# Filter rows for the upper partitions: four loads replaced by two engine copies in a kernel's prologue, and the weights' load issued earlier

## The chip, the cores and the metric

The kernel runs on one core of one Trainium2 chip. The metric is the device time in microseconds; lower is better. A run's time is some 1.8 us longer than the span of its profile (783.67 against 781.9 us in the profile). Times before come from runs of 782.77 to 784.03 us.

## The reference

```python
def _attn_ref(x, filt_r, filt_i):          # x: 8 x 3008 x 256
    X = np.fft.rfft(x, axis=1)
    Y = X * (filt_r + 1j * filt_i)[None]
    return np.fft.irfft(Y, n=x.shape[1], axis=1).astype(np.float32)

def _moe_ref(x, w_in, w_out):              # 24064 x 256, 256 x 2048, 2048 x 256
    h = x @ w_in
    return (np.maximum(0.01 * h, h) @ w_out).astype(np.float32)

# reference: _moe_ref(_attn_ref(x, ...).reshape(24064, 256), ...)
```

A filter along the sequence by Fourier transform, then two dense layers with a leaky ReLU between.

## The kernel before

The transforms are matmuls with small constant matrices in several stages: first stage, a transpose on the vector engine (STREAM_TRANSPOSE in the profiles, single ones of 128x1024 took 1.22 and 1.25 us), second stage, product with the filter, third stage, a second transpose, fourth stage. The dense layers follow. The batches 1 to 7 are transformed while the dense layers of an earlier batch run. Only batch 0 stands alone: it is the **prologue**, some 42 us in which TensorE has nothing else to do. Batch 0 is worked in two halves of 128 columns (`hf`).

The filter lies in `fa_sb` (real part) and `fb_sb` (imaginary part). Both halves of the partitions need the same rows, so rows 0 to 63 ("lower") are repeated in 64 to 127 ("upper"). For half 0 two engine copies do that (`upper(0)`); for half 1 the kernel before loads the rows from DRAM a second time. In code and profiles, PE is TensorE, DVE or `dve` the vector engine, ACT or `act` the scalar engine, Pool the GpSimd engine and SP SyncE, which here only issues DMAs. A load "lands" when its data has arrived.

```python
    def filt_load(dst, src, d0, dn, up=0):
        for q, first, sgn in ((0, 0, 1), (Q, N1, -1)):
            nc.gpsimd.dma_start(dst[up + q : up + q + Q, :, ds(d0, dn)], ...)
    ...
    for hf in range(2):
        filt_load(fa_sb, filt_r, hf * DH, DH)
        filt_load(fb_sb, filt_i, hf * DH, DH)
    filt_load(fa_sb, filt_r, DH, DH, 64)         # upper rows of half 1
    filt_load(fb_sb, filt_i, DH, DH, 64)
    ...
    def first_s2(hf, c, n, kind, on_pool=False): # second stage and products, n columns of rows
        ps = bank(kind, n, DH)
        ...                                      # matmuls into ps
        if on_pool:
            ...                                  # ACT copies ps to SBUF, Pool multiplies
        else:
            for i in range(2):                   # by fa, then by fb
                nc.vector.tensor_tensor(y[i], ps, fs[i], AL.mult)

    def first_sa(hf, c, n=4):                    # third stage, evacuated by ACT
        ...
    def upper(hf):
        for t, cp in ((fa_sb, act), (fb_sb, dve)):
            cp(t[64:P, :, ts(hf, DH)], t[0:64, :, ts(hf, DH)])
    ...
    t1_part(0, 0, True)(), t1_part(0, 1, True)() # first transposes
    nc.vector.memset(i1_sb[:, 0, 0:2], 0.0)
    nc.sync.dma_start(i1_sb[:], i1_d.ap())       # inverse constants, 752 KB
    upper(0)
    first_s2(0, 8, 8, "ph", True)
    nc.gpsimd.dma_start(w_in_sb[:], ...)         # first-layer weights
    t1_part(0, 2, True)()
    first_s2(0, 0, 8, "ph")
    for n0 in (0, N2 // 2):
        x_load(1, n0, N2 // 2)
    t1_part(0, 3, True)()
    first_s2(0, 16, 4, "pf"), first_s2(0, 20, 4, "pf")
    keep_warm(4)                                 # idle matmuls
    first_s2(1, 0, 8, "ph")
    first_sa(0, 0, 8)
    first_s2(1, 8, 8, "ph", True)
    nc.gpsimd.dma_start(w_out_sb[:], ...)
    first_sa(0, 16), first_sa(0, 20), first_sa(0, 8, 8)
    first_s2(1, 16, 4, "pf"), first_s2(1, 20, 4, "ph")
    first_sa(1, 0, 8)
    ...                                          # rest of third stage, transposes, fourth stage
```

## Time and profile before

| | kernel before |
|---|---|
| median of 3 runs | 782.98 us (782.77 to 784.03) |
| span of the profile | 781.9 us |
| TensorE busy | 770.7 us, 99% |
| first vector transpose starts | 17.48 us |
| first dense-layer matmul starts | 42.40 us |
| from there to the end | 739.5 us |

Two marks of this table serve throughout. The first transpose of the vector engine starts when the input of batch 0 has come in and gone through the first stage, and that moment moves by itself. I call the time from the first transpose to the first dense-layer matmul the **lead-in**: 42.40 - 17.48 = 24.92 us here.

### The profile page before, as it was taken

How to read it: one execution, taken by the hardware profiler on the slowest of the kernel's cores; microseconds unless marked ns; L12 is line 12 of the kernel's file. 1: busy time of each engine (PE TensorE's matmuls, PEld its weight loads, DVE VectorE, ACT ScalarE, POOL GpSimd, SP SyncE). 2: the span in 40 equal slices, each digit the busy share in tenths (PEclk: the TensorE clock that was granted, in tenths of full speed). 3: DMA queues.
4: the chain of work that ended last, by engine and by line, in shares of the span. 5: the costliest groups of instructions: out<-in, count | busy, mean ns of one | idle time of the engine just before them, and what ended most of it. 6: DMA issues, size and time to landing. Idle time of an engine off the chain costs nothing.

```text
span 781.9 us, 13405 instructions
## 1 busy us (share of the span) xinstructions
PE 770.7 (99%) x5710; PEld 523.5 (67%) x5710; DVE 368.6 (47%) x467; ACT 550.7 (70%) x783; POOL 150.2 (19%) x124
## 2 busy tenths in 40 slices
PE   8799999999999999999999999999999999999998
PEld 4366677666776667666777667766677666766666
DVE  4879751865237641577307754087432765200000
ACT  4586769676787767777587775967668776666664
POOL 5963300340004300042001410025000340000000
PEclk9999999999999999999999999999999999999999
DMA  9973102301041101510105010140101001110111
GB/s 182 220 112 75 38 28 57 93 28 41 29 106 42 42 28 42 108 41 29 41 28 122 28 39 31 41 107 28 42 28 42 28 28 41 41 37 32 41 41 55
DMA packets 39500, 44.16 MB, mean 56 GB/s; under 512 B 11282, under 2 KB 37522, under 8 KB 38674
## 3 DMA queue, kind: packets, MB, share of 16 engines
q0 software_dynamic: 13104, 17.01, 13.2%
q1 hardware_dynamic: 26336, 26.30, 9.6%
q8 instruction: 44, 0.72, 0.4%
q14 instruction: 16, 0.13, 0.1%
HBM read 35.67 MB, written 24.64 MB: 77 GB/s over the span
## 4 chain that ended last, share of the span: by engine, by line
PE 94%; DMA 3%; ACT 1%; DVE 1%; POOL 1%; issue 0%; DVEq 0%; POOLq 0%
PE ph L377 41%; PE po_ps L391 41%; DMA fb_sb<-in_filt_i_dram 3%; PE pf L174 3%; PE pf L241 2%; PE pf L229 2%; PE pf L214 2%; PE pf L391 1%; ACT big L185 0%; DVE prod L281 0%; DVE big L296 0%; POOL x_sb L132 0%; ACT yt L308 0%; PE ph L305 0%; ACT gt_c L382 0%
## 5 line engine op out<-in xcount | busy, mean ns | idle before, releaser
L382 ACT ACTIVATE gt_c<-ph 128x1024 f16<-128x1024 f32 x376 | 385.3, 1025 | 195.3 <-PE ph L377 194.0
L377 PE MATMUL ph<-yt,w_in_sb 128*128 128x512 f16 (+3 forms) x1600 | 386.4, 366 | 0.3
L391 PE MATMUL po_ps<-w_out_sb,gt_c 128*128 128x256 f16 x2944 | 381.5, 272 | 0.5 <-ACT ost_c_t L398 0.5
L391 PEld LDWEIGHTS <-gt_c 128*128 128x128 f16 x3008 | 290.8, 98 | 89.2 <-issue 1.9
L377 PEld LDWEIGHTS <-w_in_sb 128*128 128x128 f16 x1600 | 154.5, 98 | 95.7 <-issue 0.4
L222 POOL TENSOR_TENSOR y_b_g<-p_b_g,p_b_g 128x512 f16<-128x512 f32 x84 | 106.9, 1273 | 225.0 <-DVE p_b_g L220 225.0
L197 DVE STREAM_TRANSPOSE big<-big 128x1024 f32<-128x1024 f32 x32 | 55.9, 1850 | 126.1 <-ACT big L185 126.1
L185 ACT CAST big<-pf 128x512 f16<-128x512 f32 x186 | 106.4, 603 | 1.8 <-PE pf L254 1.8
L244 DVE CAST yt<-pf 128x376 f16<-128x376 f32 x112 | 56.3, 544 | 86.1 <-PE pf L241 86.1
L218 DVE TENSOR_TENSOR p_b_g<-pf,fa_sb 128x512 f32<-128x512 f32 x84 | 58.1, 692 | 37.7 <-PE pf L214 34.9
L398 ACT COPY ost_c_t<-po_ps 128x256 f32<-128x256 f32 x184 | 69.3, 377 | 6.5 <-PE po_ps L391 5.3
L205 DVE STREAM_TRANSPOSE big<-big 128x1024 f32<-128x1024 f32 x28 | 51.0, 1934 | 34.4 <-ACT big L185 34.4
L219 DVE TENSOR_TENSOR p_b_g<-pf,fb_sb 64x512 f32<-64x512 f32 x84 | 58.2, 692 | 1.1
L220 DVE TENSOR_TENSOR p_b_g<-pf,fb_sb 64x512 f32<-64x512 f32 x84 | 57.4, 683 | 1.1
L132 POOL DMA_DIRECT2D x_sb<-in_x_dram x13 | 7.1, 546 | 254.9 <-PE pf L174 254.1
L241 PEld LDWEIGHTS <-big 128*128 128x128 f16 x448 | 25.6, 98 | 13.2
L174 PE MATMUL pf<-x_sb,f_sb 94*128 94x256 f16 x224 | 33.9, 272 | 0.2 <-DVE yt L244 0.2
L214 PE MATMUL pf<-big,small_sb 128*128 128x512 f16 x84 | 31.8, 379 | 0.0
L229 PE MATMUL pf<-y_b_g,small_sb 128*128 128x512 f16 x84 | 31.8, 379 | 0.0
L174 PEld LDWEIGHTS <-f_sb 94*128 94x128 f16 x224 | 21.5, 97 | 12.4 <-issue 0.4
L241 PE MATMUL pf<-i_sb,big 128*128 128x94 f16 x448 | 28.7, 206 | 0.0
L317 PE MATMUL po_ps<-idle 128*128 128x512 f16 x66 | 17.0, 404 | 1.2 <-DVE one L163 1.2
(49 smaller groups left out, 156.1 us busy)
## 6 DMA issues: line engine op xcount, KB each, us to landing
out_dram<-ost_c_t SPq DMA_DIRECT2D x92, 256.0 KB, 2.1
x_sb<-in_x_dram POOLq DMA_DIRECT2D x5, 1536.0 KB, 11.1
x_sb<-in_x_dram POOLq DMA_DIRECT2D x2, 768.0 KB, 14.3
x_sb<-in_x_dram POOLq DMA_DIRECT2D x3, 480.0 KB, 9.9
fa_sb<-in_filt_r_dram POOLq DMA_DIRECT2D x6, 192.0 KB, 11.9
fb_sb<-in_filt_i_dram POOLq DMA_DIRECT2D x6, 192.0 KB, 11.3
w_in_sb<-in_moe_w_in_dram POOLq DMA_DIRECT2D x1, 1024.0 KB, 9.8
w_out_sb<-in_moe_w_out_dram POOLq DMA_DIRECT2D x1, 1024.0 KB, 15.0
```

What stands on the lines that cost most here:

```text
L174: nc.tensor.matmul(ps[:, j, :], f1_sb[:N1, n2, :], x_sb[:N1, n2, :], start=True, stop=True)
L185: copy(paired(dst)[:, ds(n0, nn), ds(e0, de)], ps.rearrange("p n (e t) -> p n e t", t=2))
L218: nc.vector.tensor_tensor(p1[:], ps, fa, AL.mult)
L219: nc.vector.tensor_tensor(p2[0:64], ps[64:P], fb[64:P], AL.mult)
L220: nc.vector.tensor_tensor(p2[64:P], ps[0:64], fb[0:64], AL.mult)
L222: nc.gpsimd.tensor_tensor(y1[:], p1[:], p2[:], AL.add)
L241: nc.tensor.matmul(ps[:, j, :], src[:, dt, n2, :], i1_sb[:, n2, :], start=True, stop=True)
L244: copy(yv[:, :, ds(4 * h, 4)], ps.rearrange("p c a -> p a c"))
L377: nc.tensor.matmul(ph[:, j, ds(o, ln)], w_in_sb[:, dt, ts(ct, P)], yt[:, dt, ds(lo, ln)], start=(dt == 0), stop=(dt == NDT - 1),)
L382: nc.scalar.activation(gts[ci][:, ds(2 * g, 2), :], ph, AF.Lrelu)
L391: nc.tensor.matmul(po, gts[ci][:, ct, ts(tj, P)], w_out_sb[:, ct, :], start=(ct == 0), stop=(ct == NCT - 1))
L398: nc.scalar.copy(ost[:, tj % 2, :], po)
```

## The change

The intent: the last of the four repeated loads lands at 30.95 us and holds the vector engine up. Copy the upper rows of half 1 on chip as well, in gaps of ACT and the vector engine, and let the weights' load take the place of the repeated loads in the queue.

```diff
-    def filt_load(dst, src, d0, dn, up=0):
+    def filt_load(dst, src, d0, dn):
...
-    filt_load(fa_sb, filt_r, DH, DH, 64)
-    filt_load(fb_sb, filt_i, DH, DH, 64)
+    nc.gpsimd.dma_start(w_in_sb[:], moe_w_in.rearrange("(dt p) c -> p dt c", p=P))
...
-    def upper(hf):
-        for t, cp in ((fa_sb, act), (fb_sb, dve)):
-            cp(t[64:P, :, ts(hf, DH)], t[0:64, :, ts(hf, DH)])
+    def upper(hf, t, copy):
+        copy(t[64:P, :, ts(hf, DH)], t[0:64, :, ts(hf, DH)])
...
-    upper(0)
+    upper(0, fa_sb, act), upper(0, fb_sb, dve)
     first_s2(0, 8, 8, "ph", True)
-    nc.gpsimd.dma_start(w_in_sb[:], moe_w_in.rearrange("(dt p) c -> p dt c", p=P))
...
     t1_part(0, 3, True)()
+    upper(1, fa_sb, act)
     first_s2(0, 16, 4, "pf"), first_s2(0, 20, 4, "pf")
+    upper(1, fb_sb, dve)
     keep_warm(4)
```

More of the change, by code (lines that the diff above doesn't have):

```diff
@@ L135, in x_load @@
                         ap=[[N2 * D, cnt], [D, nn], [1, dn]]))
-    def filt_load(dst, src, d0, dn, up=0):
+    def filt_load(dst, src, d0, dn):
         for q, first, sgn in ((0, 0, 1), (Q, N1, -1)):
             nc.gpsimd.dma_start(
-                dst[up + q : up + q + Q, :, ds(d0, dn)],
+                dst[q : q + Q, :, ds(d0, dn)],
                 bass.AP(tensor=src.tensor, offset=src.offset + first * D + d0,
```

## The prediction

Its sum: 782.98 - 1.10 = 781.9, with 1.10 from 1.96 - 0.95 and 0.1 of overlaps, and the copies at their measured 0.95 and 2.75 us.

> **What bounds the kernel now.** I read the page's busy rows first, then the chain that ended last, then the timeline from 14 to 43 us, then the waits of that stretch.
>
> ```profile
> PE 770.7 (99%) x5710; PEld 523.5 (67%) x5710; DVE 368.6 (47%) x467; ACT 550.7 (70%) x783; POOL 150.2 (19%) x124
> PEclk9999999999999999999999999999999999999999
> PE ph L377 41%; PE po_ps L391 41%; DMA fb_sb<-in_filt_i_dram 3%; PE pf L174 3%; PE pf L241 2%; PE pf L229 2%; PE pf L214 2%; PE pf L391 1%; ACT big L185 0%; DVE prod L281 0%; DVE big L296 0%; POOL x_sb L132 0%; ACT yt L308 0%; PE ph L305 0%; ACT gt_c L382 0%
> ```
>
> TensorE is the bound, at full clock, and what follows the first dense-layer matmul (42.40 us) is 740 us of it. In the windows view PE is busy 723.46 of the 728 us from 54 us on. The change touches nothing there. It can only move the start of that stretch: the prologue. The one entry of the chain that isn't TensorE and is large is the load of the imaginary filter, 3%, some 25 us. In order of time (columns: start us, us, what):
>
> ```profile
> 5.59 13.82 DMA fb_sb<-in_filt_i_dram
> 19.41 0.28 issue
> 19.69 11.26 DMA fb_sb<-in_filt_i_dram
> ...
> 31.07 1.24 DVE prod L281
> 32.31 0.04 issue
> 32.35 0.59 PE ph L267
> ```
>
> So the prologue ends on the last of four loads that bring the second half's filter rows a second time, for partitions 64 to 127. It lands at 19.69 + 11.26 = 30.95 us and releases a vector product at 31.07. The timeline shows the vector engine there, with its idle time in brackets:
>
> ```profile
> 27.22 0.67 DVE L281 TENSOR_TENSOR prod<-pf,fb_sb 128x512 f16<-128x512 f32 x1
> 28.90 1.23 DVE L281 TENSOR_TENSOR prod<-ph,fa_sb 128x1024 f16<-128x1024 f32 x1 [1.01 <-DMA fa_sb<-in_filt_r_dram]
> 31.07 1.22 DVE L281 TENSOR_TENSOR prod<-ph,fb_sb 128x1024 f16<-128x1024 f32 x1 [0.95 <-DMA fb_sb<-in_filt_i_dram]
> 34.61 4.86 DVE L296 STREAM_TRANSPOSE big<-big 128x1024 f32<-128x1024 f32 x4
> ```
>
> Two waits, 1.01 + 0.95 = 1.96 us, are all the idle time of the vector engine from 17.48 to 37 us but crumbs. It is therefore the resource of this stretch. **The ceiling of the gain is 1.96 us, 0.25% of the time.**
>
> [...] The first half's copies measured 0.953 and 2.750 us, so I use those:
>
> ```profile
> 17.47 2.75 ACT L312 COPY fa_sb<-fa_sb 64x3072 f16<-64x3072 f16 x1
> 19.69 1.51 POOL L140 DMA_DIRECT2D fb_sb<-in_filt_i_dram  x1 [0.41 <-DMA fb_sb<-in_filt_i_dram]
> 19.90 0.95 DVE L312 COPY fb_sb<-fb_sb 64x3072 f16<-64x3072 f16 x1
> ```
>
> [...] the Pool issue beside this copy took 1.51 us where its like took 0.71. The new copy must therefore fall where Pool is idle.
>
> [...] Reading each issue by itself in the tile view (start plus time to landing), the eight second-half loads land at 21.87 and 22.53 (fa, lower), 23.64 and 26.65 (fb, lower), 27.69, 28.78, 29.9 and 30.95 (upper), in issue order and some 1.1 us apart, apart from one gap of 3.0 us where the 752 KB of inverse constants, issued at 19.90 on the other queue, went past.
>
> **The change, part by part.**
>
> Removed: four loads of 192 KB, four Pool issues (3 x 0.71 + 1.51 us, in a stretch where Pool waited for ACT anyway: its first product starts at 21.62 upon ACT's copy and stays there), and with them both waits of 1.96 us.
>
> Added on ACT: one 2.75 us copy after its copies of 20.95 to 22.02. The lower fa rows land at 22.53; with the 0.12 us that the trace shows from landing to start (30.95 to 31.07), it runs from 22.65 to 25.40. ACT then sat idle 5.04 us until TensorE's result at 27.07. So the copy is hidden, with 1.67 us to spare.
>
> Added on the vector engine: one 0.95 us copy after the product of 27.22. Lower fb rows landed at 26.65, so it need not wait. It runs from about 27.85 to 28.83. From the first half, the next instruction follows a copy's start by 0.99 us (19.90 to 20.89): the fa product starts at 28.85, as good as where it was (28.90). The copy takes the place of the first wait. The second wait goes: product follows product by 1.11 to 1.15 us (22.06 to 23.17, 31.07 to 32.22), so the fb product starts at about 29.97 in place of 31.07. **Gain: 1.10 us** = 1.96 of waits less 0.95 of copy, with 0.1 of overlaps.
>
> Pool during that copy: the input loads for batch 1, ahead of which the first-layer weights' issue (0.78 us) has gone, run from 26.08 to 27.13; its products start at 29.03 on ACT's copy. The vector copy falls in the gap between, so neither holds the other.
>
> Does the 1.10 us reach 42.40? TensorE's second-stage matmul at 32.35 waited 1.28 us for the fb product and moves to about 31.25; the matmul before it ends at 31.07, so it does not bind. The third-stage matmuls at 34.29 follow on TensorE without a gap; their last two need Pool's products, which end at 33.53, and would be reached at about 34.4. ACT's last copy (end 37.05) starts the third transpose at 37.09; the first two transposes follow the vector products. Both move by the same amount. The following 5.3 us are a chain of TensorE, ACT and vector copies among themselves.
>
> Moved: the first-layer weights, issued at about 16.4 in place of 26.08. They had landed at 26.08 + 9.8 = 35.9, 6.5 us before 42.40, so their being late cost nothing and being earlier gains nothing by itself. Behind the lower rows they took 4.9 us (30.95 to 35.9), so they should now land near 26.65 + 4.9 = 31.6. The second half of batch 1's input, which landed at 27.4 + 15.8 = 43.2, comes some 4 us earlier, and the second-layer weights (48.5, needed at 53.98) too. Nothing new becomes late for a start at 41.3.
>
> Sum: 782.98 - 1.10 = **781.9 us**.
>
> **The rivals.**
>
> (1) A copy waits for its lower rows, so that a new wait takes the place of the old. For it: the margin on fb is only 1.2 us (26.65 against 27.85), and 2 MB of weights in fp32 now queue directly behind. Against: the eight loads landed in issue order. If the rows came 1 us later than I read them, the gain would still be about 1; at over 2 us it is gone: 783.0.
>
> (2) Something just behind takes over: Pool's products for the second half (end 33.53), the pf matmul that ends at 31.07 just as the product wants it at 31.12, or ACT's gates on the transposes. Margins are 0.05 to 0.9 us, so this may take up to half: 782.4.
>
> (3) The prologue is hidden, or the long stretch gives it back by falling into another phase: 783.0. Against: the chain goes through the prologue, and in the waits from 42.4 us on TensorE lost only 0.7 us to named waits, so the stretch moves as a block.
>
> (4) More than my sum: earlier input and weights relieve something. The waits name no late load after 31.07, so at most a few tenths: 781.5.
>
> **Range and chances.** The gain is 0.14%; the three runs before spread over 1.26 us (782.77 to 784.03), as much as the effect. Point 781.9, range 781.2 to 783.0: the low end is the full gain of 1.96 with a little noise, the high end no gain. Neither a gain nor a loss of 2% (15.7 us) is in reach of a change that moves some four microseconds of work in the prologue: chance of faster 0.005, within 2% 0.99, slower 0.005.
>
> **What would show it.** In the profile after: no 3% entry of the filter load in the chain; the ACT copy of fa at about 22.7 in a gap before 27.1; the vector copy of fb at about 27.85, the fa product right behind at 28.85 and the fb product at about 29.97, without DMA idle before them; first third-stage transpose near 33.5 (34.61 before); first dense-layer matmul near 41.3 (42.40), and from there to the end the same 739.5 us. It would be wrong if the vector copy showed a DMA wait over 0.3 us, if the transposes moved less than the products, or if the stretch after the first dense matmul differed by over 0.5 us.

## The result

| | before | changed |
|---|---|---|
| median of 6 runs | 783.87 us (782.77 to 784.27) | 783.37 us (782.75 to 784.01) |
| ratio | | 0.9996 (0.9983 to 1.0009) |
| span of the profile | 781.9 us | 780.9 us |
| mean clock of the profile | 1.000 | 0.997 |
| first transpose | 17.48 us | 16.81 us |
| first dense-layer matmul | 42.40 us | 41.50 us |
| lead-in | 24.92 us | 24.69 us |

Ratios are the mean time of one kernel's fast runs over that of the other's in the same rounds, so not quite the ratio of the medians quoted beside them. The predicted range (781.2 to 783.0) missed the measured 783.37.

The profiled span is 1.0 us shorter, as if the prediction of 1.10 had come true. The marks say otherwise: 0.67 us of that is the first transpose starting sooner by itself, and the lead-in is only 0.23 us shorter. The busy row and the chain of the changed kernel's page:

```profile
PE 771.9 (99%) x5710; PEld 523.9 (67%) x5710; DVE 369.5 (47%) x468; ACT 553.7 (71%) x784; POOL 146.4 (19%) x120
PE 94%; ACT 1%; DVE 1%; issue 0%
```

The DMA's 3% is gone from the chain, DVE and ACT have gained a copy each (368.6 to 369.5 and 550.7 to 553.7 us), and Pool has lost its four issues. So far all is as foreseen. The timeline of the changed kernel's vector engine (start us, duration us, line, out<-in, in brackets the idle time before):

```profile
26.55 0.68 DVE L279 TENSOR_TENSOR prod<-pf,fb_sb 128x512 f16<-128x512 f32 x1
27.26 0.95 DVE L309 COPY fb_sb<-fb_sb 64x3072 f16<-64x3072 f16 x1
28.24 1.23 DVE L279 TENSOR_TENSOR prod<-ph,fa_sb 128x1024 f16<-128x1024 f32 x1
29.38 1.22 DVE L279 TENSOR_TENSOR prod<-ph,fb_sb 128x1024 f16<-128x1024 f32 x1
31.30 0.69 DVE L279 TENSOR_TENSOR prod<-pf,fa_sb 128x512 f16<-128x512 f32 x1 [0.70 <-PE pf L265]
```

Both waits for DMA have gone and the copy stands where I put it. The fb product starts 29.38 - 16.81 = 12.57 us after the first transpose, against 31.07 - 17.48 = 13.59 before: 1.02 us sooner. But the next product waits 0.70 us for TensorE. TensorE's timelines in the same place, first before, then changed:

```profile
25.58 1.02 PE L267 MATMUL ph<-big,small_sb 128*128 128x512 f16 x2 [2.07 <-DVE big L197]
26.42 1.04 PE L288 MATMUL pf<-prod,small_sb 128*128 128x512 f16 x4
27.30 1.02 PE L267 MATMUL ph<-big,small_sb 128*128 128x512 f16 x2
```

```profile
24.91 1.02 PE L265 MATMUL ph<-big,small_sb 128*128 128x512 f16 x2 [2.07 <-DVE big L195]
25.76 1.88 PE L286 MATMUL pf<-prod,small_sb 128*128 128x512 f16 x4
27.44 1.06 PE L265 MATMUL ph<-big,small_sb 128*128 128x512 f16 x2
```

The same four matmuls took 1.04 us before and 1.88 us now. The windows view shows why: the last three columns are the granted clock of TensorE (1.00 is full speed), the DMA share and GB/s. Changed kernel (27 to 28 us, clock 0.50, left out):

```profile
25.00:26.00 1.00, 1.00 (x3) 0.26 (x4) 1.00 (x3) 0.00 (x0) 1.00 (x2) 0.77 1.06 303
26.00:27.00 1.00, 1.00 (x3) 0.29 (x2) 1.00 (x3) 0.17 (x1) 0.52 (x2) 0.50 1.05 305
28.00:29.00 1.00, 1.00 (x4) 0.29 (x3) 0.97 (x2) 0.75 (x2) 0.00 (x0) 0.53 1.07 221
```

The clock was at half for some 3.4 us from 25.5 on (0.46 + 1 + 1 + 0.94 us, worked back from the clock of each microsecond: a mean of 0.77 is 0.46 us at half). I call such a stretch a clock dip. In the profile of before it was 1.00 throughout this stretch. So two questions stood: is the clock dip an effect of the change, and what would the change give without it?

### The profile page after: what moved, and what is told of

The parts are those of the page before. It is cut to its first block, busy times and chain, and to the rows that moved or that the text cites. A ratio compares the mean times of both kernels' runs of the same rounds, so it can differ in the third digit from the quotient of the medians.

```text
span 780.9 us, 13401 instructions
## 1 busy us (share of the span) xinstructions
PE 771.9 (99%) x5710; PEld 523.9 (67%) x5710; DVE 369.5 (47%) x468; ACT 553.7 (71%) x784; POOL 146.4 (19%) x120
## 4 chain that ended last, share of the span: by engine, by line
PE 94%; ACT 1%; DVE 1%; issue 0%
PE ph L375 41%; PE po_ps L389 41%; PE pf L172 3%; PE pf L239 2%; PE pf L227 2%; PE pf L212 2%; PE pf L389 1%; ACT big L183 0%; DVE prod L279 0%; PE pf L286 0%; DVE big L294 0%; PE ph L303 0%; ACT yt L306 0%; ACT gt_c L380 0%; PE ph L265 0%
```

## The experiments

Eighteen runs followed, six of them of the two kernels as they are. No run was found in the slow state; single looks (e5 to e10, e15, e16) count as of unknown state, so their times are not compared, only their profiles. Where I quote the lead-in it is (first dense-layer matmul) - (first transpose) of the run's profile.

### The two kernels again: e1, e2, e9, e10, e15, e16

No edit. e1, e9 and e15 are the kernel before; e2, e10 and e16 the changed one.

> The kernel before, unchanged, run again. The lead-in is the time from the vector engine's first transpose to the first dense-layer matmul: 42.40 - 17.48 = 24.92 us in the profile of before, 41.50 - 16.81 = 24.69 us in that of the changed kernel, where TensorE's clock was granted at half for about 3 us from 25.8 us on. Theory A (the dip comes more often with the change): this kernel's runs show a mean clock of 0.999 to 1.000 in nearly all runs and a lead-in of 24.9 us. Rival B (the dip is a matter of chance in either kernel): some of these runs show 0.997 or 0.998 as well. Ratio to before 1.000 either way.

> The changed kernel, unchanged, run again. Theory A: all runs show a mean clock of 0.997 or 0.998 and the lead-in is again 24.7 us. Rival B: some runs show 1.000, and a profile without the dip would show a lead-in of 24.92 - 1.10 = 23.8 us. Ratio to before 0.9985 to 1.000.

> The kernel before once more, for one more profile of how its loads land. Three of four profiles with the upper rows loaded showed one DMA wait of 0.84 to 0.93 us on the vector engine, and only the first one 1.01 + 0.95 us. Theory: about 0.9 us again, and a lead-in of 24.05 us without the clock dip or 24.7 us with it. Rival (the first profile was the usual case): 1.9 us of waits and 24.9 us.

> The changed kernel once more. Theory: lead-in 23.9 us without the dip or 24.7 us with it; no DMA wait on the vector engine either way.

> The kernel before once more: lead-in 24.0 to 24.1 us without the clock dip, 24.5 to 24.7 us with it, and 24.9 us only where the loads land as late as in the first profile.

> The changed kernel once more: lead-in 23.9 us without the clock dip or 24.5 to 24.7 us with it.

With the first profile of each, eight profiles:

| kernel | profile | clock dip | DMA waits of the products, us | first transpose | first dense matmul | lead-in |
|---|---|---|---|---|---|---|
| before | first | no | 1.01 + 0.95 | 17.48 | 42.40 | 24.92 |
| before | e1 | yes | 0.93 | 17.03 | 41.72 | 24.69 |
| before | e9 | yes | 0.27 | 17.85 | 42.34 | 24.49 |
| before | e15 | no | 0.23 + 0.95 | 17.86 | 42.01 | 24.15 |
| changed | first | yes | none | 16.81 | 41.50 | 24.69 |
| changed | e2 | no | none | 17.76 | 41.65 | 23.89 |
| changed | e10 | no | none | 17.73 | 41.61 | 23.88 |
| changed | e16 | yes | none | 17.54 | 42.12 | 24.58 |

Times: e1 had a median of 783.47 us (ratio 1.0, 0.9988 to 1.0013), e2 783.31 (0.9999, 0.9986 to 1.0011); before in the same rounds 783.72.

Three things follow.

First, **the dip is not the change's doing**: two of four profiles of either kernel have it, 3.40 us long in the changed kernel's first profile and in e1 and 3.42 us in e9 and e16 (worked back as above), and rival B held. The record also has the mean clock of nearly every run. In these profiles it is 0.997 or 0.998 with the dip and 1.000 without, so the runs can be counted too: 34 of 45 executions of the kernel before read 0.997 or 0.998, and 9 of 13 of the changed kernel. The dip comes in about three quarters of the executions of either.

Second, **the profile I predicted from was an unusual one**, in two ways: it had no dip, and its waits were the longest. They are 1.96 us there, and 0.93, 0.27 and 1.18 us in the next three, of which only the last has no dip. e15, this second profile of the kernel before without a dip:

```profile
28.51 1.23 DVE L281 TENSOR_TENSOR prod<-ph,fa_sb 128x1024 f16<-128x1024 f32 x1 [0.23 <-DMA fa_sb<-in_filt_r_dram]
30.68 1.23 DVE L281 TENSOR_TENSOR prod<-ph,fb_sb 128x1024 f16<-128x1024 f32 x1 [0.95 <-DMA fb_sb<-in_filt_i_dram]
31.82 0.68 DVE L281 TENSOR_TENSOR prod<-pf,fa_sb 128x512 f16<-128x512 f32 x1
```

and e10, a profile of the changed kernel without a dip:

```profile
28.17 0.95 DVE L309 COPY fb_sb<-fb_sb 64x3072 f16<-64x3072 f16 x1
29.15 1.23 DVE L279 TENSOR_TENSOR prod<-ph,fa_sb 128x1024 f16<-128x1024 f32 x1
30.29 1.21 DVE L279 TENSOR_TENSOR prod<-ph,fb_sb 128x1024 f16<-128x1024 f32 x1
31.43 0.68 DVE L279 TENSOR_TENSOR prod<-pf,fa_sb 128x512 f16<-128x512 f32 x1
```

From the first transpose, the fb product starts at 30.68 - 17.86 = 12.82 us with the loads and at 30.29 - 17.73 = 12.56 us with the copies. The copy costs the vector engine 0.98 us (28.17 to 29.15), and the waits it takes away were worth about 1.2. The change swaps one for the other; 0.26 us remain, and the lead-ins differ by just that (24.15 and 23.88).

Third, the means of the four lead-ins, 24.56 and 24.26 us, differ by 0.30 us. The ratio 0.9996 of the first series is 0.31 us. The two agree, but four profiles are few, and the ratio's interval (0.9983 to 1.0009) has room for anything from a gain of 1.3 us to a loss of 0.7.

My expectation for e9 named about 0.9 us of waits; it had 0.27, and then 1.26 us of waiting for a TensorE that ran at half clock:

```profile
29.66 1.23 DVE L281 TENSOR_TENSOR prod<-ph,fb_sb 128x1024 f16<-128x1024 f32 x1 [0.27 <-DMA fb_sb<-in_filt_i_dram]
32.14 0.69 DVE L281 TENSOR_TENSOR prod<-pf,fa_sb 128x512 f16<-128x512 f32 x1 [1.26 <-PE pf L267]
```

So in the profiles with the dip the loads hardly matter: the next product waits for TensorE, with the loads (0.8 us in e1, 1.26 in e9) as with the copies (the 0.70 us above, 0.59 in e16).

### Filling TensorE's idle stretch: e3, e4

TensorE sits idle for 2.07 us ahead of half 1's first matmul (the bracket in the lines above), in both kernels. Eight more idle matmuls fill it; on the changed kernel (e3) and on the one before (e4).

```diff
-    keep_warm(4)
+    keep_warm(12)
```

> The changed kernel with eight more idle matmuls (12 for 4) in the place where TensorE sat idle for 2.07 us before the second half's first matmul. They need 8 x 0.22 = 1.7 us, so they fit. Theory A or B alike (idle TensorE lets the clock drop, and the dip takes 0.8 us back): clock 0.999 to 1.000 in all runs, no slow matmuls, lead-in 23.8 us, and 0.8 us faster than the changed kernel. Rival C (the dip has nothing to do with that idle time): clock again 0.997 or 0.998, lead-in 24.7 us.

> The kernel before with the same eight idle matmuls more. Theory A: lead-in 24.9 us and the time of before, as it had no dip to lose. Rival B: runs on average up to 0.5 us faster than before, as the dip goes from those runs that had it. Clock 0.999 to 1.000 in all runs in both.

No dip in either. e3: lead-in 23.89 us, median 782.97 us, ratio 0.9991 (0.9979 to 1.0004). e4: lead-in 24.05 us, median 783.07 us, ratio 0.9996 (0.9983 to 1.001). In the same rounds the unfilled ones had 783.31 (e2) and 783.47 (e1). Both fall by 0.3 to 0.4 us. That suits the clocks of these runs: e2 had the dip in two of five, at a cost of 0.7 to 0.8 us of lead-in (24.69 - 23.89 and 24.58 - 23.88), and e1 in four of five, at 0.4 to 0.6 us (24.49 and 24.69 against 24.05), though no interval here is narrow enough to prove it. I had expected 24.9 us for e4's lead-in under theory A; it had 24.05, the first sign that the first profile's 24.92 was no fair base. With the dip out of the way in both, the change is worth 24.05 - 23.89 = 0.16 us.

The filling was kept for all later versions but e11. Of ten profiles so filled (e3 to e8, e13, e14, e17, e18) none has a dip in this place, and all 34 runs of these kernels read a mean clock of 0.999 or 1.000.

### More idle time: e11

```diff
-    keep_warm(4)
```

> The changed kernel with the four idle matmuls of that place taken out, so that TensorE's idle stretch grows from 2.07 to about 2.9 us. Theory (an idle stretch of TensorE makes the clock dip[...]): a dip to half for about 3 us at the matmuls behind it, lead-in 24.7 us or more, mean clock 0.997 or 0.998, time 783.4 us or more. Rival (chance): no dip and 23.9 us.

The idle stretch grew to 2.94 us, and the dip came: half clock from 25.0 to about 28.4 us (3.42 us), lead-in 24.69 us. The time, median 783.14 us over 4 runs (ratio 0.9999, 0.9984 to 1.0015), doesn't show it; I had expected 783.4 or more. The profiled run began its first transpose at 16.53 us, the earliest of all, which by itself is worth a microsecond. All four runs read 0.995 to 0.998. That the idle stretch brings the dip rests on these counts of runs: none of 34 with the stretch filled, 43 of 58 with 2.07 us of idle time (34 of 45 and 9 of 13), four of four with 2.94 us. That a longer stretch brings it more often is not shown (four of four is not clear of 43 of 58), and why 2.07 us bring it in some executions and not in others is open.

### What the upper rows cost at most: e5

The changed kernel with the fill, but with half 1's upper rows neither loaded nor copied. The result is wrong; a zero tile fills the rows early, where ACT idles.

```diff
+    for t in (fa_sb, fb_sb):
+        for c in range(0, NC, 4):
+            nc.scalar.copy(t[64:P, ds(c, 4), ts(1, D // 2)], idle[64:P].rearrange("p (c d) -> p c d", c=4))
...
-    upper(1, fa_sb, act)
-    upper(1, fb_sb, dve)
```

> Wrong result on purpose: the changed kernel with the eight idle matmuls more, and with the second half's upper filter rows neither loaded nor copied (they are filled from a zero tile by ACT long before, between 2 and 10 us). Without a clock dip the lead-in was 23.89 us with both copies (two profiles) and 24.05 us with the loads (one profile). Theory D (the path behind the vector products is already set by TensorE and ACT: the matmul into pf that ended at 31.36 just before the product that reads it at 31.46): lead-in 23.8 to 23.9 us, so the 0.95 us copy costs almost nothing and taking it away gives almost nothing. Rival E (the vector engine alone sets the path): lead-in 23.89 - 0.99 = 22.9 us.

Lead-in 42.13 - 18.29 = 23.84 us: 0.05 us less than with both copies. The vector engine's time is simply waited away one product later (vector engine, then TensorE, of e5):

```profile
29.76 1.21 DVE L282 TENSOR_TENSOR prod<-ph,fb_sb 128x1024 f16<-128x1024 f32 x1
31.92 0.69 DVE L282 TENSOR_TENSOR prod<-pf,fa_sb 128x512 f16<-128x512 f32 x1 [0.95 <-PE pf L268]
```

```profile
30.80 0.59 PE L289 MATMUL pf<-prod,small_sb 128*128 128x512 f16 x2 [0.36 <-ACT big L290]
31.29 0.59 PE L268 MATMUL pf<-big,small_sb 128*128 128x512 f16 x1
```

The fb product now starts at 29.76 - 18.29 = 11.47 us from the first transpose, 1.1 us sooner than in e10. The next product reads a `pf` bank, and its matmul (31.29) stands in TensorE's queue behind six third-stage groups, which wait for ACT to empty the banks (0.36 us in the lines above). Theory D held: this gate, 0.05 us behind the changed kernel's vector engine, caps everything that may be done to the upper rows. The kernel before, at 24.05 to 24.15 us without the dip, was 0.2 to 0.3 us away from that cap.

### What delays the loads: e6

The kernel before with the fill and the inverse constants (752 KB, on SyncE's queue) issued later.

```diff
-    nc.vector.memset(i1_sb[:, 0, 0:2], 0.0)
-    nc.sync.dma_start(i1_sb[:], i1_d.ap())
...
     t1_part(0, 3, True)()
+    nc.vector.memset(i1_sb[:, 0, 0:2], 0.0)
+    nc.sync.dma_start(i1_sb[:], i1_d.ap())
```

> The kernel before with the eight idle matmuls more, and the 752 KB of inverse constants issued some 5 us later (at about 25.5), behind the last of the upper filter rows. Theory F (the constants held the upper rows back by about 2 us in the gap of 3.0 us between two landings): the eight second-half loads land some 1.1 us apart without a gap, the last at about 27.5 us, no DMA wait before any vector product, lead-in 23.8 to 23.9 us as TensorE and ACT then set it. Rival: the gap stays somewhere in the eight loads, a wait of about 0.9 us stays, lead-in 24.05 us.

The eight second-half loads landed at 21.02, 22.13, 23.27, 24.34, 25.43, 26.58, 27.66 and 28.73 us: 1.07 to 1.15 us apart, the gap gone. (From the first transpose, 18.16 us, the last landed at 10.6 us; in e15 at 30.51 - 17.86 = 12.65.) No vector product waits for DMA; the vector engine waits 0.93 us for TensorE's `pf` matmul in their place, as in e5. So the constants going past on the other queue cost the upper rows some 2 us, and the waits go without any copy if these two lines move. The lead-in was 24.00 us in place of 23.8 to 23.9: the first half's vector copy took 1.13 us for 0.95, beside a Pool issue (20.23 to 20.94 us), ahead of all else on the path; that this is the missing 0.15 us is argued, not tested.

### The parts alone: e7, e8

e7 adds the early weights alone to e4 (behind the repeated loads, which stay). e8 is e3 with the weights back in their old place, so the copies alone.

```diff
 e7, on the kernel before with keep_warm(12):
     filt_load(fb_sb, filt_i, DH, DH, 64)
+    nc.gpsimd.dma_start(w_in_sb[:], moe_w_in.rearrange("(dt p) c -> p dt c", p=P))
...
     first_s2(0, 8, 8, "ph", True)
-    nc.gpsimd.dma_start(w_in_sb[:], moe_w_in.rearrange("(dt p) c -> p dt c", p=P))
```

> One part of the change alone, upon the kernel before with the eight idle matmuls more: the first-layer weights issued ahead of Pool's products, directly behind the upper rows, which are loaded as before. Theory: nothing, as the weights were never late: weights land near 35 us or somewhat sooner, DMA wait before the fb product about 0.9 us, lead-in 24.05 us (up to 24.9 if this execution has the further delay of 1.1 us that the first profile of before had). Rival: the earlier issue by itself gives 0.15 us or more.

> The other part alone: the upper rows copied by ACT and the vector engine, the first-layer weights issued at their old place behind Pool's first products. Eight idle matmuls more. Theory: all that the change gives: no DMA wait, lead-in 23.9 us as with the whole change (23.89). Rival: the weights' place matters, lead-in 24.05 us or more.

e7: a wait of 0.84 us before the fb product, lead-in 24.06 us (24.05 without the part). e8: no wait, lead-in 23.90 us (23.89 with the whole change). The copies are all of the change; the weights' place is worth nothing, as they were never late.

### Taking the gate away: e12, e13, e14

If TensorE's order is the cap, then changing it should make the vector engine's copy count. In half 1, let Pool's share come first, and put the last eight columns of rows as one group into the wide bank that ACT empties soon, ahead of the third-stage groups. e14 is that alone, on e3:

```diff
+    first_s2(1, 8, 8, "ph", True)
     first_s2(1, 0, 8, "ph")
     first_sa(0, 0, 8)
-    first_s2(1, 8, 8, "ph", True)
     nc.gpsimd.dma_start(w_out_sb[:], ...)
+    first_s2(1, 16, 8, "ph")
     first_sa(0, 16), first_sa(0, 20), first_sa(0, 8, 8)
-    first_s2(1, 16, 4, "pf"), first_s2(1, 20, 4, "ph")
     first_sa(1, 0, 8)
...
-    first_sa(1, 16), first_sa(1, 20), first_sa(1, 8, 8)
+    first_sa(1, 8, 8), first_sa(1, 16), first_sa(1, 20)
```

e12 and e13 have that order and no vector copy in half 1: ACT copies the fb rows, and the fa rows come by a DMA from SBUF to SBUF on SyncE's queue (e12) or by loads right behind the lower rows (e13). Both issue the inverse constants later, as e6 does.

```diff
 e12:
-    nc.vector.memset(i1_sb[:, 0, 0:2], 0.0)
-    nc.sync.dma_start(i1_sb[:], i1_d.ap())
+    nc.sync.dma_start(fa_sb[64:P, :, ts(1, DH)], fa_sb[0:64, :, ts(1, DH)])
...
     t1_part(0, 3, True)()
-    upper(1, fa_sb, act)
+    nc.vector.memset(i1_sb[:, 0, 0:2], 0.0)
+    nc.sync.dma_start(i1_sb[:], i1_d.ap())
+    upper(1, fb_sb, act)
...
-    upper(1, fb_sb, dve)
 e13, where it differs from e12:
-    nc.sync.dma_start(fa_sb[64:P, :, ts(1, DH)], fa_sb[0:64, :, ts(1, DH)])
...
-    for hf in range(2):
-        filt_load(fa_sb, filt_r, hf * DH, DH)
-        filt_load(fb_sb, filt_i, hf * DH, DH)
+    filt_load(fa_sb, filt_r, 0, DH)
+    filt_load(fb_sb, filt_i, 0, DH)
+    filt_load(fb_sb, filt_i, DH, DH)
+    filt_load(fa_sb, filt_r, DH, DH)
+    filt_load(fa_sb, filt_r, DH, DH, 64)
```

> A version that should beat both: the changed kernel with the eight idle matmuls more; the upper fa rows copied by a DMA from SBUF to SBUF on the SyncE queue, the upper fb rows by ACT in its gap, so that the vector engine copies nothing; the inverse constants issued behind them; Pool's share of the second half's second stage ahead of the vector engine's, and the last eight columns as one product into the wide bank that ACT has emptied, so that no matmul of TensorE stands in the vector engine's way. Expected from the profiles: vector products without a wait, ending at about 14.9 us from the first transpose in place of 16.1; lead-in about 22.6 us against 23.9; 1.3 us faster than the changed kernel with the idle matmuls (its five runs had a median of 782.97), so 781.7, ratio to before about 0.9975. If the path through ACT and the third-stage transposes binds after all: lead-in 23.3 us or more.

e12 failed: 784.67 us, ratio 1.0015 (1.0003 to 1.0028), slower. Its profile is of the slowest of its five runs. The DMA from SBUF to SBUF, 384 KB, issued at 21.7 us, took 10.1 us to land, beside the weights; how much of that was the sharing is not separated:

```profile
31.83 1.23 DVE L279 TENSOR_TENSOR prod<-ph,fa_sb 128x1024 f16<-128x1024 f32 x1 [3.61 <-DMA fa_sb<-fa_sb]
```

With the wait of 3.61 us TensorE sat idle for 1.91 us (up to 33.12) and 0.73 us (up to 34.24), and a clock dip of 3.40 us followed at 35 to 39 us (two of the five runs had none, at a mean clock of 1.000); lead-in 44.85 - 17.79 = 27.06 us. It says nothing of the gate.

> The combined version again, without the DMA from SBUF to SBUF that took 10 us: the upper fa rows loaded as in the kernel before, but right behind the lower rows; the upper fb rows copied by ACT in its gap; the inverse constants issued later; the vector engine copies nothing, and TensorE's order changed so that no matmul gates the last vector products. Eight idle matmuls more. Theory D (TensorE's and ACT's order was the gate that hid the copy): vector products without a wait, lead-in about 22.7 us against 23.9, time about 1.2 us below the changed kernel with the idle matmuls. Rival (something else further on binds): lead-in 23.3 us or more.

> The changed kernel with the eight idle matmuls and with TensorE's new order alone: both copies as the change has them. Theory D: the copy is then on the path with its whole 0.95 us, lead-in about 23.7 us, 1.0 us more than in e13. Rival: the two are alike within 0.3 us, so the copy is hidden for another reason.

The third-stage transposes, right behind the last vector product, started at 32.28 - 17.40 = 14.88 us from the first transpose in e13 and at 33.83 - 17.47 = 16.36 us in e14: with the gate gone, the copy costs 1.48 us (the two also differ in how the fa rows come and in when the constants are issued, but the product ahead of the copy starts at 9.75 and 9.74 us in the two, and no vector product behind it waits in either). That is more than its 0.98: in e14's profile Pool's products had come forward into the copy's place (vector engine, then Pool, of e14):

```profile
27.91 1.35 DVE L309 COPY fb_sb<-fb_sb 64x3072 f16<-64x3072 f16 x1
```

```profile
27.29 2.99 POOL L276 TENSOR_TENSOR prod<-fx_h_c,fa_sb 128x512 f16<-128x512 f32 x2
```

Side by side, the copy took 1.35 us for 0.95 and Pool's pair 2.99 for 2.28. Theory D held up to there. The lead-ins, 23.67 (e13) and 24.15 us (e14), hold only a third of it, and I had expected 22.7 and 23.7. e13's missing microsecond is a wait that I had made myself:

```profile
35.69 0.69 PE L305 MATMUL pf<-i_sb,big 128*64 128x94 f16 x16 [1.06 <-DMA i_sb<-inv_const]
```

The inverse constants, issued at 25.48 us, landed at 35.6. Times: e13 782.25 us, ratio 0.9987 (0.9973 to 1.0); e14 782.88 us, ratio 0.9994 (0.9982 to 1.0007).

### The constants in time: e17, e18

e13 with the memset and the issue of the constants one step (e17) or two steps (e18) of the vector engine earlier.

```diff
 e17, on e13:
     first_s2(0, 0, 8, "ph")
+    nc.vector.memset(i1_sb[:, 0, 0:2], 0.0)
+    nc.sync.dma_start(i1_sb[:], i1_d.ap())
 e18, on e13:
     t1_part(0, 2, True)()
+    nc.vector.memset(i1_sb[:, 0, 0:2], 0.0)
+    nc.sync.dma_start(i1_sb[:], i1_d.ap())
 (both: the two lines taken out behind t1_part(0, 3, True)())
```

> As e13, the inverse constants issued at about 24.2 in place of 25.5, so that they land near 34.3 us, just before the first matmul that reads them (34.65). Lead-in 22.7 us if they are in time, up to 23.2 us if not; time about 781.5 to 782.0, ratio to before about 0.998. If something else binds behind: 23.6 us as in e13.

> As e13, the inverse constants issued at about 22.0, so that they land near 32 us, while the upper fa rows land up to 2 us later than in e13 (25.7), at most at 27.7, just before the product that reads them (27.75). Lead-in 22.7 us, or up to 0.5 us more if that product waits; ratio to before about 0.998.

e17: **781.03 us** (780.67 to 781.79), ratio 0.9972 (0.9958 to 0.9985), the first version whose interval lies below 1; before in the same rounds 783.15. Its result is correct. From its timelines, vector engine first:

```profile
28.08 1.21 DVE L281 TENSOR_TENSOR prod<-ph,fa_sb 128x1024 f16<-128x1024 f32 x1
32.61 2.35 DVE L296 STREAM_TRANSPOSE big<-big 128x1024 f32<-128x1024 f32 x2
```

```profile
40.42 0.38 PE L376 MATMUL ph<-yt,w_in_sb 128*128 128x512 f16 x1
```

The lead-in is 40.42 - 17.74 = 22.68 us, as worked out beforehand, though the second dense matmul then waited 0.28 us. e18: the last of the upper fa rows landed at 28.75 us where I had put 27.7 at most, and the product waited 1.12 us; lead-in 41.23 - 17.34 = 23.89 us, 781.88 us, ratio 0.9981 (0.9968 to 0.9993). The constants, sent at 22.0 us, cost what I had foreseen: the last two landings are 2.98 us apart (25.77 and 28.75), 1.9 more than in e17. The further 1.0 us was there before: the first half-1 load landed at 21.92 us, where e17's, issued at the same time, landed at 20.37. That is the same late first load as in the first profile (below). So this one profile doesn't tell whether e18's place for the constants is worse than e17's.

## Why the prediction was wrong

**What held.** The ACT copy lay in its gap: in e10 from 22.31 to 25.06 us, ahead of ACT's next work at 27.32. The vector copy took 0.95 us and its place was right: the fb product at 12.56 us from the first transpose, where the prediction put it at 29.97 - 17.48 = 12.49. Pool did not get in its way: in e10 the copy ran from 28.17 to 29.12 us, between the end of Pool's issues at 27.42 and the start of its products at 29.28. The weights' place was worth nothing (e7). Dip-free lead-ins of the changed kernel are 23.88 and 23.89 us; the prediction's is 24.92 - 1.10 = 23.82. For the changed kernel the working was right to 0.07 us. (Two slips in it did no harm: the 4.9 us of the weights were counted from the last of the upper rows, not the lower ones; and of the landings "some 1.1 us apart" the first two are only 0.66 us apart, a sign that the first came late.)

**What failed is the other end of the subtraction.** The step reads "1.96 of waits less 0.95 of copy, with 0.1 of overlaps". The 1.96 us came from one profile, and the step took it for the kernel. In the other profiles of that kernel without a dip it was 1.18 us (e15), 0.93 (e4) and 0.84 (e7). What is further in the first profile, 0.8 to 1.1 us, shows in its landings: between the last load of half 0 and the first of half 1 lay 2.48 us (19.39 to 21.87), where e1, e9 and e15 had 1.03 to 1.08. What held that one load up is open; it came again in e18 (some 2.6 us). From the first transpose, the last upper row landed at 13.5 us in the first profile, at 11.7 in e9 and at 12.65 in e15. With the later waits the same sum gives 0.0 to 0.3 us, and the lead-ins show 0.16 to 0.27.

**A term that was missing.** TensorE's clock falls to half for 3.4 us behind its idle stretch in about three quarters of the executions of either kernel (34 of 45 and 9 of 13, by the mean clock), and then TensorE, not the vector engine or a load, sets the path: lead-ins of 24.49 to 24.69 us with either kernel. In those executions the change is worth next to nothing. The times say so too: fast runs that read 0.997 or 0.998 have a mean of 783.47 us before (33 runs) and 783.50 changed (8); those that read 0.999 or 1.000 have 783.23 (8) and 783.03 (3), too few to prove the second difference. Some 0.2 to 0.3 us in a quarter of the executions is less than 0.1 us on average, by this estimate. The first profile of before showed full clock, and I wrote "TensorE is the bound, at full clock" and did not ask whether the 2.07 us of idle time that I saw would always be so lucky. That the first profile showed no dip was chance: only 11 of 45 executions read so.

**The rivals.** Rival 2 ("something just behind takes over", among it the pf matmul, with a margin of 0.05 us) named the right place. The loads' usual wait is only 0.2 to 0.3 us above that gate, as e5 shows, and the gate is what the dip moves. But I gave it "up to half" of a gain that wasn't there. Rival 1 (a copy that waits) didn't occur; rival 3 was the nearest in size, for another reason.

**The range** failed for a second cause besides, and in microseconds it is the larger one: of the 1.49 us between 781.88 (782.98 - 1.10) and 783.37, 0.89 are the base (783.87 for 782.98) and about 0.6 the gain (0.50 between the medians, itself not clear of noise, for 1.10). The upper end was "no gain" counted from 782.98, the median of three runs that spread over 1.26 us. In four later sets of nine runs each the kernel before had medians of 783.72, 783.46, 783.26 and 783.15 us, and 783.87 in the six runs of the result. With the true base near 783.5, even a gain of 0.3 us ends above my range. A spread as large as the effect, which I did write down, should have gone into the upper end as well.

## What to carry to other kernels

A wait in one profile is one draw: where the sum is under a microsecond, take several profiles of the kernel before, measure from a mark that cancels the start's own jitter, and only then subtract. Ask of each removed wait what stands 0.1 us behind it, and test that by removing the work altogether (e5); here the gate behind was worth more than the change, and gate, copy and clock dip taken away together, with the constants and the weights issued in other places, gave 0.28% (e17). And where TensorE idles on the path, look at its clock behind the hole in several profiles and try idle matmuls in it: here, by the mean clock, half clock came with 2.07 us of idle time in 43 of 58 executions and cost 0.4 to 0.8 us of lead-in, and came in none of the 34 with the hole filled.
